# Window attention and SiLU MLP on one core: the partition maximum of the later chunks by a DRAM line instead of GpSimd, and other step times for the folded blocks

## The chip, the cores and the metric

The kernel runs on one core of one Trainium2 chip. The metric is the device time of one execution in microseconds (us), as the median of three runs. Engines go by their names in the profile: PE is TensorE's matmul, PEld its weight load, DVE is VectorE, ACT is ScalarE, POOL is GpSimd, SP is SyncE, whose queue issues every transfer here.

## What is computed

```python
# x (4, 4096, 192), weight_gen (4, 4096, 8 heads, 7 taps)
w = softmax(weight_gen, axis=-1)
x_unf = x_pad[:, s + k, :]                      # a causal window of 7 rows, 8 heads of 24 columns
attn = np.einsum('bshk,bskhg->bshg', w, x_unf)  # (16384, 192)
h = attn @ w_in                                 # 192 -> 2048
out = (h * (1 / (1 + np.exp(-h)))) @ w_out      # 2048 -> 192
```

Everything is float32 at the inputs and the output; the matmuls work on pairs of float16 (an upper and a lower part), for which x is scaled by a power of two that is common to all 128 partitions.

## The kernel before

**Blocks and chunks.** The 16384 rows are 128 tiles of 128; four tiles make a block, so there are 32 blocks. The inputs come in ten chunks: chunks 0 and 1 hold one block, chunk 2 two, chunks 3 to 9 four each. Per chunk the kernel loads `xc` and `wc`, makes the softmax weights (`softmax_steps`) and finds the scale: `scale_steps` sums |x| on ACT in four parts into the columns of `xm` (128 partitions x 4), `absmax_over` takes the maximum over all partitions, and `x_scales` and `finish_scales` make small 128x1 tiles of it (`xup`, `inv`, `gup`, `od`) with a few DVE instructions. `absmax_over` has two steps: `over`, a GpSimd `partition_all_reduce` (L177), and `top`, a DVE maximum over the four columns (L184).

**A block.** `prep_steps` makes the weighted sum over the 7 taps: four products and three sums on POOL (three and two before block 7), the others on DVE (products L487, sums L493, tiles `pr`), then one last DVE sum that joins both halves, the float16 upper part on ACT (L460) and the lower part on DVE (L463, tile `xs`), and a transposition and two half swaps by DMA (`turned`, L470 and L455). PE then makes the first layer into PSUM (`banks`), ACT the SiLU (L732) and the upper float16 part (L743), DVE the lower part (L747, called lower here), both into a ring of 15 (`ringed`); PE makes the second layer out of the ring (L786, L790), and in blocks from 7 on ACT (L684) and POOL (L685, L686) finish each tile of the output.

**Folded blocks.** From block 7 (`FOLD`) a part of the first layer is made with fewer products out of sums: sums of the weights, made once (`fold_w`, L577 to L587, the tiles named `v_out` and `v_in`), and sums of the weighted x, made for every block (`fold_x`: four on POOL, L603, an upper part on ACT, L606, a lower part on DVE, L609, and a transposition, L613). A folded block has two halves, n = 0 and n = 1. In each, PE runs `fold_1` for two pairs of banks, `tile_sums` (second layer), `plain`, `fold_2`, `fold_3`, and `plain`; DVE adds three pieces after `fold_1` (`joined`, L677), a fourth after `fold_2`, without which `fold_3` (L656, the 18 matmuls with `v_in` and `xt` or `xu`) may not start, and makes four lowers: of the last pair of the half before, of z after the fourth joined, and of x and y.

**What sets the order.** All engines run their instructions in the order in which the program issues them. The main loop issues the matmuls, SiLUs and lowers; all the preparation is a list of steps with due times, and `drain(u)` issues whatever is due up to unit u. A block has 16 units, so a unit is some 1.94 us. The table `START` gives the due times: the steps of block b count from u0 = 16 (b - 2), those of a chunk from the u0 of its first block. A folded block drains at its units 0, 1, 2, 3, 5, 6, 7 and 8, 9, 10, 11, 13, 14, 15, so a step due at 12.5 is issued at 13.

- `any_x`: four parts of |x|, `over`, `top`, `x_scales`, the rest of the scales (chunks 4 to 9; `first_x` is the one of chunk 3).
- `fold_v`: DVE product, product, sum, product, sum, joining sum, then ACT upper, DVE lower, transposition.
- `fold_p`: POOL product, product, sum, product, sum, product, sum.
- `fold_s`: the four sums of `fold_x`, upper, lower, transposition. `fold_w`: fetch, four POOL sums, then five pairs of upper and lower.

Of the kernel before, what the change touches and what calls it, by code (L numbers as in the profile page):

```python
# [10 lines left out]
F32 = mybir.dt.float32  # L11
# [3 lines left out]
ALU = mybir.AluOpType  # L15
AX = mybir.AxisListType

P = 128
# [27 lines left out]
    "b2v": (13.1,) * 1 + (13.2,) + (13.3,) * 3 + (13.4,) * 4 + (13.45,) + (19,) + (21,) * 2 + (23, 23, 23),  # L46
    "first_s": (-2, 1, 4, 6.2, 6.5, 8.5),
    "first_x": (-4, -1, 1, 9, 9.25, 18, 19, 20),
    "any_s": (-32, -32, -23, -16, -14, -10),
    "c4s": (-32, -32, -19, -16, -13, -10),  # L50
    "any_x": (-39, -30, -15, -6, -4.5, 3, 4, 5),
    "early": (-5, -41),
    "b3v": (11, 11, 13, 13, 15, 17, 17, 18, 19, 20.5, 20.5, 21, 21, 22.5, 23, 23),
    "b4v": (10, 12, 13, 14.5, 16, 17, 18.5, 20, 22.5, 23, 23),
    "any_p": (11.25,) * 5,
    "any_v": (11, 11.5, 13, 14, 15, 17, 18.5, 20, 22.5, 23, 23),
    "fold_v": (8, 9, 10, 12, 14, 16, 17, 19, 19),
    "fold_p": (1, 3, 5, 7, 9, 11, 13),
    "fold_s": (16.5, 16.5, 16.5, 16.5, 18, 20, 20),
    "fold_w": (36, 44, 45, 46, 47, 50, 52, 53, 55, 58, 60, 61, 63, 64, 65),  # L60
    "prep": (12.5,),
    "load": (0,),
}
# [14 lines left out]
FOLD = 7  # L78
# [6 lines left out]
def kernel(  # L85
# [19 lines left out]
    nc = tc.nc  # L105
# [35 lines left out]
    sm_p = ctx.enter_context(tc.tile_pool(name="sm", bufs=2))  # L141
# [29 lines left out]
    def absmax_over(m, name):  # L171

        got = {}

        def over():
            got["mb"] = sm_p.tile([P, 4], F32, tag="mb", name=f"mb_{name}")
            nc.gpsimd.partition_all_reduce(got["mb"][:, 0:m.shape[1]], m, P, bass_isa.ReduceOp.max)  # L177

        def top():
            if m.shape[1] == 1:  # L180
                got["all"] = got["mb"][:, 0:1]
                return
            r = sm_p.tile([P, 1], F32, tag="ra", name=f"ra_{name}")
            nc.vector.tensor_reduce(out=r, in_=got["mb"][:, 0:m.shape[1]], op=ALU.max, axis=AX.X)  # L184
            got["all"] = r

        return got, [over, top]

# [4 lines left out]
    def x_scales(got, c):  # L193

        p2 = sc_p.tile([P, 1], I32, tag="p2", name=f"p2_{c}")
        down = sc_p.tile([P, 1], F32, tag="xdown", name=f"xdown{c}")
        up = sc_p.tile([P, 1], F32, tag="xup", name=f"xup{c}")
        bits(p2, got["all"].bitcast(I32), EXPONENT, ALU.bitwise_and)
        bits(down, p2.bitcast(F32), FLOOR, ALU.max, 1.0 / TOP_X, ALU.mult)
        nc.vector.reciprocal(out=up, in_=down)  # L200
        sc[c, "down"], sc[c, "up"] = down, up
# [132 lines left out]
    def load_x(c):  # L334
        t0, n = chunks[c]
        rows = HALO + n
        if c != 1:
            t = xc_p.tile([P, CT + HALO, D], F32, tag="xc", name=f"xc{c}")
        if t0 == 0:

            cut = (P - 1) // 16 * 16
            cuts = (HALO, HALO - 2, TB // 2, 0)

            def halo(hi, lo):
                nc.sync.dma_start(out=t[1:1 + cut, lo:hi, :], in_=xf[0:cut, T - HALO + lo:T - HALO + hi, :])
                nc.sync.dma_start(out=t[1 + cut:P, lo:hi, :], in_=xf[cut:P - 1, T - HALO + lo:T - HALO + hi, :])
            nc.sync.dma_start(out=t[:, HALO:rows, :], in_=xf[:, 0:n, :])
            for hi, lo in zip(cuts[:-2], cuts[1:-1]):  # L350
                halo(hi, lo)
            step["halo"] = lambda: halo(*cuts[-2:])
            nc.gpsimd.memset(t[0:1, 0:HALO, :], 0.0)

            def zeros(lo, hi):
                for q in (PB, 2 * PB):
                    nc.gpsimd.memset(t[q:q + 1, lo:hi, :], 0.0)
                q = 3 * PB
                row = t[q:q + 1, lo:hi, :].rearrange("p t d -> p (t d)")
                nc.scalar.activation(out=row, in_=zero[q:q + 1, 0:1].to_broadcast([1, (hi - lo) * D]), func=AF.Copy)  # L360
            step["zeros"] = zeros
            x_t[1] = t[:, TB:, :]
        elif c == 1:
            t = x_t[1]
            nc.sync.dma_start(out=t[:, HALO:rows, :], in_=xf[:, t0:t0 + n, :])
        else:
            nc.sync.dma_start(out=t[:, 0:rows, :], in_=xf[:, t0 - HALO:t0 + n, :])
        x_t[c] = t

    def load_w(c, queue=nc.sync):  # L370
        t0, n = chunks[c]
        t = wc_p.tile([P, CT * H, K], F32, tag="wc", name=f"wc{c}")
        queue.dma_start(out=t[:, 0:n * H, :].rearrange("p a k -> p (a k)"),
                          in_=wf[:, t0:t0 + n, :].rearrange("p t a -> p (t a)"))
        w_t[c] = t
# [32 lines left out]
    def scale_steps(c, absmax):  # L408
        t0, n = chunks[c]
        parts = n // TB  # L410
        rows = n + HALO
        cuts = [rows * i // parts for i in range(parts + 1)]
        m = sm_p.tile([P, 4], F32, tag="xm", name=f"xm{c}")

        def part(i):
            def f():
                part = x_t[c][:, cuts[i]:cuts[i + 1], :].rearrange("p t d -> p (t d)")
                if c in SUMMED:
                    abs_sum(part, m[:, i:i + 1])
                    return  # L420
                nc.vector.tensor_reduce(out=m[:, i:i + 1], in_=part, op=ALU.max, axis=AX.X,
                                        apply_absolute_value=True)
            return f

        got, chain = absmax(m[:, 0:parts], f"x{c}")

        def small():
            x_scales(got, c)

        return [part(i) for i in range(parts)], chain + [small]  # L430
# [4 lines left out]
    def finish_scales(c):  # L435
        inv = sc_p.tile([P, 1], F32, tag="inv", name=f"inv{c}")
        gup = sc_p.tile([P, 1], F32, tag="gup", name=f"gup{c}")
        bits(inv, sc[c, "down"], wsc["down", "I"], ALU.mult)
        bits(gup, sc[c, "up"], wsc["up", "I"], ALU.mult, gtop(c) / TOP_X, ALU.mult)
        sc[c, "inv"], sc[c, "gup"] = inv, gup  # L440

    def out_scale(c):
        od = sc_p.tile([P, 1], F32, tag="od", name=f"od{c}")
        bits(od, sc[c, "inv"], wsc["down", "O"], ALU.mult, TOP_X / gtop(c), ALU.mult)
        sc[c, "od"] = od
# [64 lines left out]
    def abs_sum(v, out):  # L510
        nc.scalar.activation(out=junk_of(v.shape[1]), in_=v, func=AF.Abs, accum_out=out)
# [340 lines left out]
    def at(u, f):  # L852
        todo.append((u, len(made), f))
        made.append(f)
# [7 lines left out]
    def chain(name, fs, u0=0):  # L862
        steps = START[name][-len(fs):]
        for u, f in zip(steps, fs):
            at(u0 + u, f)

    win, wout = moe_w_in.bitcast(I32), moe_w_out.bitcast(I32)
    with tc.manual_schedule():
# [94 lines left out]
        def x2_size():  # L963
            abs_sum(x_t[2][:, 0:HALO + chunks[2][1], :].rearrange("p t d -> p (t d)"), xs2)
            got, (over, top) = absmax_over(xs2, "x2")
            over()
            step["z2"] = lambda: (top(), x_scales(got, 2), finish_scales(2), out_scale(2))
# [21 lines left out]
        for c in range(2, NC):  # L989
            u0 = (chunks[c][0] // TB - 2) * NF  # L990

            def load(c=c):
                if c > 2:
                    load_w(c)
                load_x(c)
            at(START["load"][0] if c == 2 else (chunks[c - 1][0] // TB - 1) * NF + 1, load)

            def prepare(c=c, u0=u0):
                steps = softmax_steps(c, nc.vector if c == 3 else nc.gpsimd)
                parts, more = scale_steps(c, absmax_over)  # L1000
                more.append(lambda: (finish_scales(c), out_scale(c)))
                which = "any_" if chunks[c - 1][1] == CT else "first_"
                chain("c4s" if c == 4 else which + "s", steps, u0)
                chain(which + "x", parts + more, u0)
            if c > 2:
                at(u0 + START["early"][chunks[c - 1][1] == CT], prepare)
# [10 lines left out]
        for b in range(2, NB):  # L1017
            u0 = (b - 2) * NF

            def prep(b=b, u0=u0):  # L1020
                fold = b >= FOLD
                pool, steps, last, more = prep_steps(b, 0 if b < 4 else 4 if fold else 3, fold)
                if b > 2:
                    chain("fold_p" if fold else "any_p", pool, u0)
                chain("fold_v" if fold else f"b{b}v" if b < 5 else "any_v", steps + last, u0)
                if fold:
                    chain("fold_s", more, u0)
            at(START["prep"][0] if b == 2 else u0 - 1, prep)
# [90 lines left out]
        last = (FOLD - 1, NP - 1)  # L1119
        for b in range(FOLD, NB):  # L1120
            for n in range(2):
# [31 lines left out]
                last = (b, NQ + 2 * n + 1)  # L1153
# [6 lines left out]
        for v in range(NP * (NB - 1), NP * NB):  # L1160
            b, p = pairs[v]
# [41 lines left out]
```

## Time and profile before

| | |
|---|---|
| median of 3 runs | 1094.44 us (1093.11 to 1096.25) |
| the profiled execution | 1095.73 us |
| its span, first to last instruction | 1093.9 us |
| busy: PE, DVE, ACT, POOL | 94%, 76%, 75%, 56% of the span |
| mean granted TensorE clock | 0.975 of full speed |

The profiled execution is 1.3 us longer than the median, and 1.8 us of it lie outside the span. Busy shares are averages over the start, 25 folded blocks and the end, whose limits differ.

### The profile page before, as it was taken

Reading aid. Unit: us, or ns where it says so; the run is one execution under the profiler, and the core shown is the slowest. Engines: PE = TensorE matmul, PEld = TensorE weight load, DVE = VectorE, ACT = ScalarE, POOL = GpSimd, SP = SyncE. Lnnn points to the kernel's source line nnn. Section 1 sums busy time; section 2 is a strip of 40 time slices with the busy share of each in tenths; the row PEclk is TensorE's granted clock in tenths of the full one; section 3 lists DMA queues with packets and bytes.
Section 4 is the critical chain, followed back from the end, with each engine's and each line's share of the span. In section 5 each row is a group of like instructions: output and inputs, shape, how many; then the busy total and the mean of one; then the engine's idle time right before and its main releaser. Section 6 shows DMA issues by size and latency. Waiting matters only on the chain.

```text
span 1093.9 us, 32481 instructions
## 1 busy us (share of the span) xinstructions
PE 1033.5 (94%) x14392; PEld 732.2 (67%) x14392; DVE 836.6 (76%) x905; ACT 822.7 (75%) x875; POOL 611.8 (56%) x532
## 2 busy tenths in 40 slices
PE   9999899989997999979999799997999969999998
PEld 7798677657674666646666466664666647666666
DVE  8889777768885887948878488785797848888653
ACT  7988577657985779857798478985789847777774
POOL 1000633567774678756687566874667747667320
PEclk9999999989998999989999899998999989999999
DMA  9442311225220252203432046220442302223200
GB/s 243 136 141 65 132 31 46 45 57 160 64 47 25 57 160 64 53 20 72 145 64 65 8 89 128 64 64 17 122 94 57 64 20 53 65 56 65 65 16 23
DMA packets 103335, 81.06 MB, mean 74 GB/s; under 512 B 78749, under 2 KB 93722, under 8 KB 102170
## 3 DMA queue, kind: packets, MB, share of 16 engines
q1 hardware_dynamic: 103194, 78.99, 29.5%
q8 instruction: 112, 1.84, 0.7%
q14 instruction: 29, 0.24, 0.1%
HBM read 27.85 MB, written 12.58 MB: 37 GB/s over the span
## 4 chain that ended last, share of the span: by engine, by line
PE 68%; DVE 15%; ACT 7%; issue 7%; POOL 2%; POOLq 0%; DVEq 0%; ACTq 0%
PE banks L720 21%; PE banks L786 16%; PE banks L656 12%; PE banks L790 8%; PE banks L761 5%; DVE ringed L747 4%; DVE banks L677 4%; ACT banks L732 4%; DVE pr L493 3%; ACT ringed L743 3%; DVE pr L487 2%; PE banks L711 2%; PE banks L773 2%; DVE xv L677 1%; POOL pr L493 1%
## 5 line engine op out<-in xcount | busy, mean ns | idle before, releaser
L790 PE MATMUL banks<-wo,ringed 64*128 64x192 f16 x3312 | 408.5, 243 | 40.8 <-DVE ringed L747 40.8
L786 PE MATMUL banks<-wo,ringed 64*128 64x384 f16 x3312 | 421.0, 323 | 0.0
L747 DVE SCALAR_TENSOR_TENSOR ringed<-banks,gup,ringed 128x1024 f16<-128x1024 f32 x248 | 317.0, 1279 | 105.4 <-ACT ringed L743 104.9
L732 ACT ACTIVATE banks<-banks,inv 128x1024 f32<-128x1024 f32 x248 | 269.0, 1085 | 112.0 <-PE banks L720 87.2
L743 ACT ACTIVATE ringed<-banks,gup 128x1024 f16<-128x1024 f32 x248 | 276.1, 1113 | 7.9
L720 PEld LDWEIGHTS <-w 64*128 64x128 f16 x2664 | 150.7, 96 | 133.3 <-issue 26.5
L786 PEld LDWEIGHTS <-ringed 64*128 64x128 f16 x3312 | 176.1, 94 | 90.8
L685 POOL TENSOR_TENSOR v_in<-v_in 128x384 f32<-128x384 f32 x100 | 103.2, 1032 | 197.7 <-ACT v_in L684 197.7
L790 PEld LDWEIGHTS <-ringed 64*128 64x128 f16 x3312 | 176.1, 94 | 48.9 <-DVE ringed L747 42.7
L720 PE MATMUL banks<-xt,w 64*128 64x512 f16 x1332 | 192.9, 388 | 11.6 <-DVE ringed L747 11.4
L487 POOL TENSOR_TENSOR pr<-xc,wc 128x768 f32<-128x768 f32 x109 | 171.2, 1573 | 36.4 <-DVE pr L493 28.6
L720 PE MATMUL banks<-xu,w 64*128 64x512 f16 x1332 | 191.4, 386 | 0.0
L493 POOL TENSOR_TENSOR pr<-pr,pr 128x768 f32<-128x768 f32 x81 | 161.5, 1994 | 49.0 <-issue 43.1
L493 DVE TENSOR_TENSOR pr<-pr,pr 128x768 f32<-128x768 f32 x105 | 123.6, 1177 | 57.9 <-POOL pr L493 56.4
L677 DVE TENSOR_TENSOR banks<-banks,xv 128x512 f32<-128x512 f32 x150 | 104.0, 694 | 66.1 <-PE banks L656 60.5
L684 ACT ACTIVATE v_in<-banks,od 128x768 f32<-128x768 f32 x100 | 89.6, 896 | 69.7 <-PE banks L790 67.5
L487 DVE TENSOR_TENSOR pr<-xc,wc 128x768 f32<-128x768 f32 x108 | 137.5, 1277 | 0.2
L656 PE MATMUL banks<-xu,w 64*128 64x256 f16 (+1 forms) x600 | 135.7, 324 | 0.5 <-DVE ringed L747 0.3
L656 PE MATMUL banks<-xt,w 64*128 64x256 f16 (+1 forms) x600 | 135.7, 324 | 0.0
L656 PEld LDWEIGHTS <-w 64*128 64x128 f16 x1500 | 103.8, 95 | 31.6
L656 PEld LDWEIGHTS <-v_in 64*128 64x128 f16 x1200 | 85.3, 95 | 31.9 <-issue 8.6
L686 POOL TENSOR_TENSOR o<-v_in 128x192 f32<-128x192 f32 x100 | 100.8, 1008 | 7.9
(123 smaller groups left out, 978.2 us busy)
## 6 DMA issues: line engine op xcount, KB each, us to landing
xc<-in_x_dram SPq DMA_DIRECT2D x7, 2112.0 KB, 9.7
xu<-xt SPq DMA_DIRECT2D x62, 192.0 KB, 2.9
out_dram<-o SPq DMA_DIRECT2D x61, 192.0 KB, 2.3
v_out<-v_out SPq DMA_DIRECT2D x50, 128.0 KB, 2.5
wc<-in_weight_gen_dram SPq DMA_DIRECT2D x7, 448.0 KB, 4.0
ringed<-in_moe_w_out_dram SPq DMA_DIRECT2D x8, 384.0 KB, 9.3
ringed<-in_moe_w_in_dram SPq DMA_DIRECT2D x14, 192.0 KB, 8.4
xc<-in_x_dram SPq DMA_DIRECT2D x1, 1344.0 KB, 10.1
```

Source lines behind the costliest of these rows:

```text
L487: eng.tensor_tensor(out=pr[k].rearrange("p t (h g) -> p (t h) g", g=G), in0=xin, in1=wv, op=ALU.mult)
L493: eng.tensor_tensor(out=pr[k], in0=pr[k], in1=pr[l], op=ALU.add)
L656: nc.tensor.matmul(h, w, x, start=start, stop=False, skip_group_check=True)
L677: nc.vector.tensor_tensor(out=to, in0=quarter[:, :, in0], in1=kept[:, :, in1], op=ALU.add)
L685: nc.gpsimd.tensor_tensor(out=s[:, 0], in0=s[:, 0], in1=s[:, 1], op=ALU.add)
L686: nc.gpsimd.tensor_tensor(out=o[:, t], in0=s[:, 0, 0:D], in1=s[:, 0, D:2 * D], op=ALU.add)
L720: nc.tensor.matmul(h[:, i], w16[rows, part, p, g], x_in[rows, :, k, :], start=n == 0, stop=n == NT9 - 1)
L732: nc.scalar.activation(out=h, in_=h, func=AF.Silu, scale=sc[chunk_of[b], "inv"])
L743: nc.scalar.activation(out=g_t[b, p][:, 0], in_=h_t[b, p], func=AF.Copy, scale=sc[chunk_of[b], "gup"])
L747: nc.vector.scalar_tensor_tensor(out=g[:, 1], in0=h_t.pop((b, p)), scalar=sc[chunk_of[b], "gup"], in1=g[:, 0], op0=ALU.mult, op1=ALU.subtract)
L786: nc.tensor.matmul(acc_t[b, t, i], gh_t[b, f][rows, t * P:(t + 1) * P], wo16[rows, place(f)], start=f == 0, stop=False, skip_group_check=True)
L790: nc.tensor.matmul(acc_t[b, t, i][:, 0, :], gl_t[b, f][rows, t * P:(t + 1) * P], wo16[rows, place(f), 0], start=False, stop=False, skip_gr ...
```

## The change

For chunks 3 to 9 the maximum over partitions no longer uses GpSimd. SP writes `xm` (128 x 4 floats) to a line in DRAM, and a second transfer reads the whole line of 512 floats back into every partition (`ml`); `top` is a DVE maximum over those 512. In `any_x` the step `top` stands 17.5 units behind `over`, and not 7.5 as before. Chunks 1 and 2 keep GpSimd. The other edits are due times; block 7 gets a list of its own (`fold_1`) for what `fold_v` lists for the later ones. `fold_w`'s POOL sums go from units 44 to 47 to units 58 to 66, its upper and lower parts from 50 to 65 to 81 to 95.

```diff
-    "any_s": (-32, -32, -23, -16, -14, -10),
+    "any_s": (-32, -32, -23, -15, -14, -10),
-    "any_x": (-39, -30, -15, -6, -4.5, 3, 4, 5),
+    "any_x": (-39, -31, -13, -5.5, -4.0, 13.5, 13.5, 15),
-    "fold_v": (8, 9, 10, 12, 14, 16, 17, 19, 19),
-    "fold_p": (1, 3, 5, 7, 9, 11, 13),
-    "fold_s": (16.5, 16.5, 16.5, 16.5, 18, 20, 20),
-    "fold_w": (36, 44, 45, 46, 47, 50, 52, 53, 55, 58, 60, 61, 63, 64, 65),
+    "fold_1": (9, 9, 11, 13, 14, 14, 14, 19, 19),
+    "fold_v": (5, 7, 9, 11, 12.5, 14.5, 17, 19, 19),
+    "fold_p": (0.5, 3.5, 5, 7, 9, 11, 14),
+    "fold_s": (14.5, 16.5, 16.5, 16.5, 18, 23, 23),
+    "fold_w": (36, 58, 60, 62, 66, 81, 81, 84, 86, 87, 88, 90, 93, 94, 95),
...
+    lines = ctx.enter_context(tc.tile_pool(name="line", bufs=2, space=bass.MemoryType.DRAM))
+    def absmax_by_line(m, name):
+        got = {}
+        def over():
+            line = lines.tile([P, 4], F32, tag="line", name=f"line_{name}")
+            n = m.shape[1]
+            got["all_of"] = sm_p.tile([P, P, 4], F32, tag="ml", name=f"ml_{name}", bufs=1)
+            nc.sync.dma_start(out=line[:, 0:n], in_=m)
+            nc.sync.dma_start(out=got["all_of"].rearrange("p q n -> p (q n)"),
+                              in_=line.rearrange("q n -> (q n)").partition_broadcast(P))
+        def top():
+            got["all"] = sm_p.tile([P, 1], F32, tag="ra", name=f"ra_{name}")
+            nc.vector.tensor_reduce(out=got["all"], in_=got["all_of"].rearrange("p q n -> p (q n)"), op=ALU.max, axis=AX.X)
+        return got, [over, top]
...
-                parts, more = scale_steps(c, absmax_over)
+                parts, more = scale_steps(c, absmax_over if c < 3 else absmax_by_line)
...
-                chain("fold_v" if fold else f"b{b}v" if b < 5 else "any_v", steps + last, u0)
+                chain("fold_1" if b == FOLD else "fold_v" if fold else f"b{b}v" if b < 5 else "any_v", steps + last, u0)
```

On POOL, at the place of chunk 5's maximum (end of block 9), before: `mb` is the all-reduce's result, `pr_0` POOL's running sum, and a bare ISA row sets GpSimd's configuration.

```order
L685 TENSOR_TENSOR v_in<-v_in 128x384
L686 TENSOR_TENSOR o_5032<-v_in 128x192
L487 TENSOR_TENSOR pr_1_4923<-xc_1779,wc_1777 128x768
L177 ISA
L177 ISA mb_x_5351<-xm_4145 128x4
L493 ISA
L493 TENSOR_TENSOR pr_0_4922<-pr_0_4922,pr_1_4923 128x768
L685 TENSOR_TENSOR v_in<-v_in 128x384
L686 TENSOR_TENSOR o_5032<-v_in 128x192
```

The same place after the change:

```order
L508 TENSOR_TENSOR pr_1_4931<-xc_1779,wc_1777 128x768
L514 TENSOR_TENSOR pr_0_4930<-pr_0_4930,pr_1_4931 128x768
L706 TENSOR_TENSOR v_in<-v_in 128x384
L707 TENSOR_TENSOR o_5037<-v_in 128x192
L624 TENSOR_TENSOR v_out<-pr_2_4932 128x2x64
```

The all-reduce and the two configuration rows are gone; the sum of `pr_0` follows its product at once.

On DVE, in half n = 0 of a folded block, where no step of a chunk lies between, from the last two joined (L677) to the first step of half n = 1, before: `pr_2` and `pr_3` are DVE's product tiles, `xs` the lower part of x, `v_out` that of the sums.

```order
L677 TENSOR_TENSOR banks<-banks,xv 128x2x256 x2
L463 SCALAR_TENSOR_TENSOR xs_3877<-pr_2_3875,xup_3545,xs_3877 128x4x192
L747 SCALAR_TENSOR_TENSOR ringed<-banks,gup_3555,ringed 128x1024
L609 SCALAR_TENSOR_TENSOR v_out<-v_out,xup_3545 128x2x256
L747 SCALAR_TENSOR_TENSOR ringed<-banks,gup_3555,ringed 128x1024 x2
L487 TENSOR_TENSOR pr_2_4400<-xc_1779,wc_1777 128x768
```

The same after the change (L698 is joined, L768 a lower, L508 a product, L630 the lower part of the sums):

```order
L698 TENSOR_TENSOR banks<-banks,xv 128x2x256 x2
L484 SCALAR_TENSOR_TENSOR xs_3879<-pr_2_3877,xup_3868,xs_3879 128x4x192
L768 SCALAR_TENSOR_TENSOR ringed<-banks,gup_3881,ringed 128x1024
L508 TENSOR_TENSOR pr_2_4408<-xc_1779,wc_1777 128x768
L768 SCALAR_TENSOR_TENSOR ringed<-banks,gup_3881,ringed 128x1024 x2
L630 SCALAR_TENSOR_TENSOR v_out<-v_out,xup_3868 128x2x256
L508 TENSOR_TENSOR pr_3_4409<-xc_1779,wc_1777 128x768
```

The first product stands where the lower part of the sums stood, between the lowers of z and x, and that part has moved behind the lower of y.

On DVE, in half n = 1 of the same block, from the lower of the last pair to the lower of y, before:

```order
L747 SCALAR_TENSOR_TENSOR ringed<-banks,gup_3555,ringed 128x1024
L677 TENSOR_TENSOR banks<-banks,xv 128x2x256
L677 TENSOR_TENSOR xv<-banks,xv 128x2x256
L677 TENSOR_TENSOR banks<-banks,xv 128x2x256
L487 TENSOR_TENSOR pr_3_4401<-xc_1779,wc_1777 128x768
L493 TENSOR_TENSOR pr_2_4400<-pr_2_4400,pr_3_4401 128x768
L677 TENSOR_TENSOR banks<-banks,xv 128x2x256
L747 SCALAR_TENSOR_TENSOR ringed<-banks,gup_3555,ringed 128x1024
L487 TENSOR_TENSOR pr_3_4401<-xc_1779,wc_1777 128x768
L747 SCALAR_TENSOR_TENSOR ringed<-banks,gup_3555,ringed 128x1024
L493 TENSOR_TENSOR pr_2_4400<-pr_2_4400,pr_3_4401 128x768
L747 SCALAR_TENSOR_TENSOR ringed<-banks,gup_3555,ringed 128x1024
```

After the change:

```order
L768 SCALAR_TENSOR_TENSOR ringed<-banks,gup_3881,ringed 128x1024
L698 TENSOR_TENSOR banks<-banks,xv 128x2x256
L698 TENSOR_TENSOR xv<-banks,xv 128x2x256
L698 TENSOR_TENSOR banks<-banks,xv 128x2x256
L514 TENSOR_TENSOR pr_2_4408<-pr_2_4408,pr_3_4409 128x768
L698 TENSOR_TENSOR banks<-banks,xv 128x2x256
L508 TENSOR_TENSOR pr_3_4409<-xc_1779,wc_1777 128x768
L768 SCALAR_TENSOR_TENSOR ringed<-banks,gup_3881,ringed 128x1024
L514 TENSOR_TENSOR pr_2_4408<-pr_2_4408,pr_3_4409 128x768
L768 SCALAR_TENSOR_TENSOR ringed<-banks,gup_3881,ringed 128x1024 x2
L514 TENSOR_TENSOR pr_2_4408<-pr_2_4408,pr_0_4406 128x768
```

A product has gone from ahead of the fourth joined (the fourth L677, now L698) to half n = 0; the third product stands ahead of the lower of z, and only a sum is left between the lowers of z and y.

## Rows read from the trace of the kernel before

**Rows 1.** Stretches: length, busy of PE, PEld, DVE, ACT, POOL; granted clock; DMA, GB/s.

```profile
344.20:378.00 33.80, 26.03 (x326) 16.19 (x328) 23.54 (x28) 18.64 (x19) 23.12 (x20) 0.85 0.22 52
378.00:411.80 33.80, 33.69 (x473) 23.09 (x470) 28.53 (x28) 27.41 (x29) 22.24 (x20) 1.00 0.44 130
...
351.90:357.40 5.50, 5.50 (x36) 2.47 (x38) 1.90 (x3) 2.35 (x3) 5.42 (x7) 0.50 0.10 36
```

**Rows 2.** POOL in order of time, end of block 9: start us, us, what, idle before.

```profile
332.00 1.54 POOL L487 TENSOR_TENSOR pr<-xc,wc 128x768 f32<-128x768 f32 x1
339.37 0.39 POOL L177 PARTITION_ALL_REDUCE mb_x<-xm  x1 [5.83 <-ACT v_in L684]
347.04 1.79 POOL L493 TENSOR_TENSOR pr<-pr,pr 128x768 f32<-128x768 f32 x1 [7.29 <-issue]
```

**Rows 3.** Waits: who for whom, us in total, times, longest.

```profile
DVE pr L493 <- POOL pr L493: 56.4, 6, 10.3
...
PE banks L790 <- DVE ringed L747: 40.8, 5, 8.6
...
PE banks L720 <- DVE ringed L747: 11.4, 3, 4.8
...
ACT v_in L583 <- POOL v_out L577: 5.8, 1, 5.8
```

**Rows 4.** Chain that ended last, folded blocks: start us, us, what.

```profile
270.12 1.80 PE banks L656 x18
...
374.09 1.80 PE banks L656 x18
...
405.15 1.80 PE banks L656 x18
...
1006.68 1.80 PE banks L656 x18
...
1034.05 1.94 PE banks L720 x18
...
1064.67 1.94 PE banks L720 x18
```

**Rows 5.** The same chain, before the folded blocks.

```profile
135.86 3.64 PE banks L720 x18
...
223.66 4.03 PE banks L720 x18
```

**Rows 6.** DVE in order of time, both halves of a folded block.

```profile
392.32 1.10 DVE L609 SCALAR_TENSOR_TENSOR v_out<-v_out,xup 128x512 f16<-128x512 f32 x1
...
395.13 1.28 DVE L747 SCALAR_TENSOR_TENSOR ringed<-banks,gup,ringed 128x1024 f16<-128x1024 f32 x1 [0.52 <-ACT ringed L743]
...
402.85 1.63 DVE L493 TENSOR_TENSOR pr<-pr,pr 128x768 f32<-128x768 f32 x1
404.41 0.69 DVE L677 TENSOR_TENSOR banks<-banks,xv 128x512 f32<-128x512 f32 x1
```

**Rows 7.** All DVE products and sums: duration ns least, median, most.

```profile
L487 DVE TENSOR_TENSOR pr<-xc,wc x108: 937/952/2584, 21.4 to 1008.4; 128x768 f32<-128x768 f32 x108
...
L493 DVE TENSOR_TENSOR pr<-pr,pr x105: 893/958/2449, 23.9 to 1013.9; 128x768 f32<-128x768 f32 x105
```

**Rows 8.** DVE groups: count, busy us, mean ns of one, idle before.

```profile
L384 DVE TENSOR_REDUCE wm<-wc 128x128 f32<-128x896 f32 x7 | 7.5, 1074 | 0.0
...
L184 DVE TENSOR_REDUCE ra_x<-mb_x 128x1 f32<-128x4 f32 x7 | 1.0, 149 | 0.0
```

**Rows 9.** Transfers: count, KB each, median us from issue to landing.

```profile
xu<-xt SPq DMA_DIRECT2D x62, 192.0 KB, 2.9
...
v_out<-v_out SPq DMA_TRANSPOSE x25, 3.6
...
xc<-in_x_dram SPq DMA_DIRECT2D x3, 22.5 KB, 3.2
```

**Rows 10.** DVE in order of time, before the folded blocks.

```profile
200.70 4.58 DVE L487 TENSOR_TENSOR pr<-xc,wc 128x768 f32<-128x768 f32 x2
```

## The prediction

> **What bounds the kernel now.** I read the stretches first, to see where PE is not busy. In the second stretch of [rows 1] PE is busy 33.69 of 33.80 us at a granted clock of 1.00: there matmuls are the bound. In the first, as long and next to it, PE is busy 26.03 us and the clock is 0.85. The reader is to see that the kernel is PE-bound except in stretches that come back once per chunk. The waits say who stops PE in them: the matmuls of the second layer waited 40.8 us in five waits for DVE's lowers, and the first layer 11.4 us in three [rows 3].
>
> POOL in order of time shows why DVE is late [rows 2]. POOL ends a product at 333.5, stands 5.83 us, runs the all-reduce in 0.39 us, stands another 7.29 us in which it waited for nothing that the profile shows ("issue"), and begins its running sum at 347.04: 13.5 us for 0.39 us of work, with a configuration row on either side of it in the order. DVE's joining sum needs that running sum; DVE waited so six times, 56.4 us in all, at most 10.3 [rows 3]. DVE is in order, so the lowers and joined pieces behind the sum wait too, and the ring and PSUM run dry for PE. After PE's gap the granted clock is 0.50, the 1.2 GHz level, in the stretch from 351.90 to 357.40 [rows 1], which makes the gap dearer than its length.
>
> The chain prices all that without my having to add gaps and clock. Between 374.09 and 405.15 the same piece of `fold_3` comes back after 31.06 us: an undisturbed block. From 270.12 to 1006.68, 22 blocks later, it took 736.56 us, and 22 x 31.06 = 683.3, so **the five maxima in between cost 53.2 us** [rows 4]. Before the folded blocks the three gaps are 11.4 us, and two first-layer groups behind them took 3.64 and 4.03 instead of 1.94 us [rows 3 to 5], another 3.8: **15.2 us** around the maxima of chunks 3 and 4.
>
> **The change, part by part.**
>
> *The all-reduce and both reconfigurations leave POOL's queue for chunks 3 to 9.* In the order POOL's sum now follows its product at once, so the 13.5 us go and with them the five disturbances: -53.2 us. Of the early 15.2 us not all comes back. One part was a wait of ACT for `fold_w`'s POOL sums (5.8 us, [rows 3]), which stood behind chunk 3's maximum; the sums now have 15 units or more to the first use. But some DVE work there is merely crowded: two products in one piece took 4.58 us [rows 10] instead of twice 0.95, and five lower parts of `fold_w` move into that stretch. I leave 3 us of the 15.2 there (bounds 0 and all 15.2), an estimate: about one such excess of 4.58 - 1.9 = 2.7 us. So -12.2 us.
>
> *The way through DRAM is added.* The write is 2 KB in 128 rows, for which the nearest row is the smallest transfer shown, 22.5 KB in 3.2 us; the read-back fills 256 KB, nearest 192 KB in 2.9 [rows 9]. SP has to wait for the first to land before it issues the second, so I take 6 us, 7 at most. `over` is issued at unit 13 of a block and `top` at unit 14 of the next, 17 units or 33 us later (a unit is 31.06 / 16 = 1.94 us). The cover is those 33 us of other blocks' work; without it seven times 6 us would be 42 us. Behind the two transfers SP has only the store of a half block's output, and the next transposition of x is due 6 units (11.6 us) on: cost 0, bound above 0 as long as the trip stays under 11 us.
>
> *`top` is longer.* 512 elements instead of 4: by the row of 896 elements, 1074 ns, some 0.61 us against 0.149 [rows 8], +0.46 us, 3.2 us over seven chunks. Most of it falls in DVE's idle time (28.5 of 33.8 us busy, [rows 1]), but it stands between two lowers; I take +1 us (0 to 3.2).
>
> *Moved steps in n = 1.* At the end of the run, where nothing is left to prepare, two halves take 1064.67 - 1034.05 = 30.62 us [rows 4], the price of the matmuls. The undisturbed block is 0.44 us longer. Part of it is in view: DVE's sum at 402.85 and the fourth joined, which ends at 405.10 [rows 6], stand right before `fold_3` at 405.15. After the change a product less stands ahead of that joined, and one product less between the lowers of z and y. 23 blocks prepare something, so the bounds are 0 and -10.1 us; I take 0.3 us a block, -6.9 us, because the sum keeps its place.
>
> *Moved steps in n = 0.* A product takes the place of the lower part of the sums (1.10 us) ahead of the lowers of x and y, and the lower of y had 0.52 us to spare, waiting for ACT [rows 6]. A product takes 0.95 us at the median and 2.58 at most, a sum 0.96 and 2.45 [rows 7]: I take no loss (bounds: no loss, and 1.0 us per block, the longest product less the part that leaves and the spare).
>
> *The rest costs nothing.* The ACT parts of |x| stay in the same gaps between `keep` and the next SiLU, or move by one drain. The transposition of the sums goes from unit 21 to 23 as issued, and is needed at 32: 17.5 us for a transposition of 3.6 and swaps of 2.9 us [rows 9].
>
> *Sum.* 1095.73 (the profiled run, span and what lies around it) - 53.2 - 12.2 + 0 + 1 - 6.9 = 1024.4. The median of the runs is 1.3 us below that run: **1023 us**.
>
> **A rule against it.** The all-reduce itself is 0.39 us [rows 2]. The Trainium skill, GPSIMD Engine Reference, section 4.1 (Engine selection), gives reductions over partitions to GpSimd and names VectorE as what not to use for them. By that rule the move would gain only the busy time, 7 x 0.39 = 2.7 us, off a queue that isn't the bound, and the time would stay between 1092 and 1094. The trace speaks against it here: the reduction is cheap and what stands around it is dear. That result is part of the second rival below.
>
> **The rivals.**
>
> 1. *DVE gets crowded in n = 0.* For it: products that run beside POOL's already take up to 2.58 us, and POOL no longer pauses 13 us per chunk. If every moved product met that, the lower of y would be about 1.0 us late in each block: 23 us, and nothing is gained in n = 1. Time 1023 + 6.9 + 23 = 1053; with half the blocks 1041. Against it: the median product is 0.95 us, so most meet nothing. 12%.
> 2. *The change doesn't do what it says.* The stops stay because something else ends as late, ACT's four sums of |x| or the softmax, whose steps surround the maximum, and what is gained is POOL's 0.39 us per chunk at most [rows 2]. Then 1092 to 1095. Against it: the three other blocks of each chunk hold the same steps and take 31.06 us. 2%.
> 3. *Slower: DVE becomes the bound of the folded blocks.* It has 28.53 / 33.80 x 31.06 = 26.2 us of work in an undisturbed block [rows 1]. If its three products and three sums of a block all went from their median to their longest, 3 x (2.58 - 0.95) + 3 x (2.45 - 0.96) = 9.4 us [rows 7], the work would be 35.6 us, 4.6 us above the block: 105 us in 23 blocks, 1023 + 6.9 + 105 = 1135. It decides from 71 / 23 = 3.1 us lost per block. Against it: POOL would have to be busy whenever DVE is, and it was busy 22.24 of 33.80 us [rows 1]. 3%.
>
> **How the numbers follow.** 83% for the forecast, whose own range is 1014 to 1032: the low end takes all of 15.2 and 10.1 and no cost of `top` (1095.73 - 1.3 - 53.2 - 15.2 - 10.1 = 1016), and the runs' spread of 2 us; the high end nothing in n = 1 and all 3.2 us. The range up to 1042 takes in rival 1 for half of the blocks. A measurement of this kernel tells about 0.3%, 3.3 us, from no change. Faster by more than that is the forecast and rival 1, 95%; within it is most of rival 2, 2%; slower is rival 3, 3%.
>
> **What would show it.** Right: POOL has one reconfiguration in the run, after chunk 2's maximum, DVE's wait for POOL's sum is gone, PE's waits for lowers fall from 52 us to a few, no stretch at 0.50 after the start, and `fold_3` comes back after 30.6 to 31.1 us in every block. Wrong: lowers that end late behind a product in n = 0, blocks above 31.1 us throughout, or `top` waiting for its transfer.

## The result, and the profile after

The changed kernel takes **1027.51 us** (median of four runs, 1027.18 to 1027.53) against 1093.78 (four runs, 1091.87 to 1096.25) beside it on the same chip: ratio 0.9392, 95% interval 0.9372 to 0.9412. The prediction was 1023 us, range 1014 to 1042. The profiled execution took 1027.18 us; its span is 1025.4 us, the mean granted clock 1.00, PE is busy 99% of the span, DVE 83%, ACT 80%, POOL 61%.

Line numbers behind the insertion are 21 higher than before: joined is L698, a lower L768, products L508, sums L514, the pieces of the folded first layer L677, the plain first layer L741, the second layer L807 and L811. `top` is L206, the small scale steps are L212 and L221.

The same two stretches as in [rows 1], after (same columns):

```profile
344.20:378.00 33.80, 33.09 (x478) 23.63 (x474) 29.17 (x35) 26.03 (x28) 24.26 (x21) 1.00 0.52 143
378.00:411.80 33.80, 33.80 (x480) 22.45 (x478) 28.18 (x28) 29.63 (x31) 27.64 (x23) 1.00 0.25 54
```

PE is busy 33.09 us in the first, not 26.03, and up to the last matmul the granted clock is nowhere below 1.00. POOL in order of time at the end of block 9, the place of [rows 2]:

```profile
334.58 1.54 POOL L508 TENSOR_TENSOR pr<-xc,wc 128x768 f32<-128x768 f32 x1
336.20 2.41 POOL L514 TENSOR_TENSOR pr<-pr,pr 128x768 f32<-128x768 f32 x1
```

The running sum follows its product 0.08 us later; before, 13.5 us lay between them. The waits that answer to [rows 3]:

```profile
PE banks L677 <- DVE ringed L768: 3.5, 5, 0.7
PE banks L741 <- DVE ringed L768: 3.3, 4, 2.1
...
PE banks L677 <- DVE banks L698: 1.1, 5, 0.2
```

DVE's wait for POOL's sum (56.4 us) is gone, and PE's waits for lowers fall from 52.2 to 6.8 us. Two of these three rows are five waits each, one per chunk, in front of the folded matmuls: new, small, and met again below. The chain, where [rows 4] stood:

```profile
304.66 1.80 PE banks L677 x18
...
320.15 1.62 PE banks L677 x18
...
335.46 1.62 PE banks L677 x18
...
350.77 1.62 PE banks L677 x18
...
366.97 1.62 PE banks L677 x18
...
799.79 1.80 PE banks L677 x18
...
996.34 1.94 PE banks L741 x18
```

These rows let the gain be split. An undisturbed block takes 350.77 - 320.15 = 30.62 us, the price of the matmuls; it was 31.06. Four chunks take 799.79 - 304.66 = 495.13 us, 123.78 each, which is 1.30 us above four undisturbed blocks. The 22 blocks that took 736.56 us in [rows 4] take 5 x 123.78 + 2 x 30.62 = 680.1 us now: **-56.4 us**. The last first-layer group of the chain stands at 996.34 instead of 1064.67, -68.33 us, so the start and the end gave **-11.9 us**.

The way through DRAM, and SP's issues of it for chunk 5:

```profile
ml_x<-line_x SPq DMA_DIRECT2D x7, 256.0 KB, 4.1
...
line_x<-xm SPq DMA_DIRECT2D x7, 2.0 KB, 2.6
```

```profile
318.74 0.34 SPq L200 DMA_DIRECT2D line_x<-xm  x1
320.37 0.33 SPq L201 DMA_DIRECT2D ml_x<-line_x  x1
```

At 2.6 + 4.1 = 6.7 us the trip has landed 31 us before `top` asks for it. Where the 1.30 us per chunk go, DVE in order of time shows, first in block 9 and then in block 10 (L416 are the softmax sums, L420 and L421 the step with the reciprocal), and under it PE in order of time at both places:

```profile
301.26 1.08 DVE L416 TENSOR_REDUCE ws<-wc 128x128 f32<-128x896 f32 x1
302.37 0.66 DVE L420 TENSOR_SCALAR ws<-ws 128x128 f32<-128x128 f32 x1
303.06 0.95 DVE L421 RECIPROCAL ws<-ws 128x128 f32<-128x128 f32 x1
303.93 0.67 DVE L698 TENSOR_TENSOR banks<-banks,xv 128x512 f32<-128x512 f32 x1
...
354.95 1.27 DVE L768 SCALAR_TENSOR_TENSOR ringed<-banks,gup,ringed 128x1024 f16<-128x1024 f32 x1
356.14 0.67 DVE L206 TENSOR_REDUCE ra_x<-ml_x 128x1 f32<-128x512 f32 x1
...
357.22 0.16 DVE L221 RECIPROCAL xup<-xdown 128x1 f32<-128x1 f32 x1
357.30 1.28 DVE L768 SCALAR_TENSOR_TENSOR ringed<-banks,gup,ringed 128x1024 f16<-128x1024 f32 x1
```

```profile
304.66 0.27 PE L677 MATMUL banks<-xu,v_in 64*128 64x256 f16 x1 [0.22 <-DVE banks L698]
...
358.64 0.27 PE L677 MATMUL banks<-xu,w 64*128 64x256 f16 x1 [0.71 <-DVE ringed L768]
```

In block 10, 1.16 us of `top` and small steps stand between two lowers, PE waits 0.71 us for the second, and the period is 366.97 - 335.46 = 31.51 us, 0.89 too long. In block 9 three softmax instructions stand ahead of the fourth joined, PE waits 0.22 us for it, and the chunk loses the other 1.30 - 0.89 = 0.41 us.

### The profile page after: what moved, and what is told of

Same layout as the page of the kernel before. It is cut to its first block, busy times and chain, and to the rows that moved or that the text cites. A ratio compares the mean times of both kernels' runs of the same rounds, so it can differ in the third digit from the quotient of the medians.

```text
span 1025.4 us, 32480 instructions
## 1 busy us (share of the span) xinstructions
PE 1011.7 (99%) x14392; PEld 732.4 (71%) x14392; DVE 851.7 (83%) x905; ACT 823.6 (80%) x875; POOL 627.6 (61%) x525
## 4 chain that ended last, share of the span: by engine, by line
PE 90%; DVE 6%; ACT 2%; issue 1%; DMA 0%; DVEq 0%; ACTq 0%
PE banks L741 26%; PE banks L807 24%; PE banks L677 16%; PE banks L811 12%; PE banks L782 6%; PE banks L732 2%; PE banks L794 2%; DVE ringed L768 2%; DVE banks L698 1%; ACT banks L753 1%; ACT ringed L764 1%; DVE pr L508 1%; PE banks L555 1%; DVE ws L416 1%; DVE xv L698 0%
## 5 line engine op out<-in xcount | busy, mean ns | idle before, releaser
L807 PE MATMUL banks<-wo,ringed 64*128 64x384 f16 x3312 | 419.8, 322 | 0.0
L811 PE MATMUL banks<-wo,ringed 64*128 64x192 f16 x3312 | 407.7, 243 | 0.1
L768 DVE SCALAR_TENSOR_TENSOR ringed<-banks,gup,ringed 128x1024 f16<-128x1024 f32 x248 | 315.9, 1277 | 68.3 <-ACT ringed L764 68.2
L508 POOL TENSOR_TENSOR pr<-xc,wc 128x768 f32<-128x768 f32 x109 | 192.0, 1764 | 91.4 <-DVE wc L424 58.9
L807 PEld LDWEIGHTS <-ringed 64*128 64x128 f16 x3312 | 177.8, 94 | 89.3
L741 PEld LDWEIGHTS <-w 64*128 64x128 f16 x2664 | 149.9, 94 | 114.9 <-issue 4.8
L706 POOL TENSOR_TENSOR v_in<-v_in 128x384 f32<-128x384 f32 x100 | 106.1, 1061 | 193.9 <-ACT v_in L705 193.9
L741 PE MATMUL banks<-xt,w 64*128 64x512 f16 x1332 | 185.0, 376 | 3.5 <-DVE ringed L768 3.3
L741 PE MATMUL banks<-xu,w 64*128 64x512 f16 x1332 | 184.9, 376 | 0.0
L811 PEld LDWEIGHTS <-ringed 64*128 64x128 f16 x3312 | 177.7, 94 | 6.3 <-DVE ringed L768 0.4
L514 POOL TENSOR_TENSOR pr<-pr,pr 128x768 f32<-128x768 f32 x81 | 177.2, 2188 | 6.3
L698 DVE TENSOR_TENSOR banks<-banks,xv 128x512 f32<-128x512 f32 x150 | 104.0, 694 | 80.2 <-PE banks L677 74.7
L508 DVE TENSOR_TENSOR pr<-xc,wc 128x768 f32<-128x768 f32 x108 | 150.6, 1398 | 0.2
L677 PE MATMUL banks<-xu,w 64*128 64x256 f16 (+1 forms) x600 | 135.0, 322 | 3.5 <-DVE ringed L768 3.5
L677 PE MATMUL banks<-xt,w 64*128 64x256 f16 (+1 forms) x600 | 135.0, 322 | 0.0
L677 PEld LDWEIGHTS <-w 64*128 64x128 f16 x1500 | 103.9, 94 | 29.5
L514 DVE TENSOR_TENSOR pr<-pr,pr 128x768 f32<-128x768 f32 x105 | 120.2, 1145 | 0.6
L677 PEld LDWEIGHTS <-v_in 64*128 64x128 f16 x1200 | 86.3, 94 | 27.6 <-issue 6.3
L677 PE MATMUL banks<-v_out,v_in 64*128 64x256 f16 x900 | 99.3, 269 | 0.0
```

The lines of the kernel that those rows point to most:

```text
L508: eng.tensor_tensor(out=pr[k].rearrange("p t (h g) -> p (t h) g", g=G), in0=xin, in1=wv, op=ALU.mult)
L514: eng.tensor_tensor(out=pr[k], in0=pr[k], in1=pr[l], op=ALU.add)
L677: nc.tensor.matmul(h, w, x, start=start, stop=False, skip_group_check=True)
L698: nc.vector.tensor_tensor(out=to, in0=quarter[:, :, in0], in1=kept[:, :, in1], op=ALU.add)
L706: nc.gpsimd.tensor_tensor(out=s[:, 0], in0=s[:, 0], in1=s[:, 1], op=ALU.add)
L741: nc.tensor.matmul(h[:, i], w16[rows, part, p, g], x_in[rows, :, k, :], start=n == 0, stop=n == NT9 - 1)
```

## The experiments

The theory: what counts is POOL's 13.5 us per maximum with the engines queued behind it, and it is gone by the way through DRAM alone; the new times give 0.44 us per folded block and take 1.3 us per chunk. The rivals: that it is the new times that moved POOL's sum out of the way; that the cover of the trip isn't needed; that the all-reduce could have stayed on GpSimd elsewhere in its queue.

### The way through DRAM alone, and the times alone

The first kernel is the changed one with all old due times, those of the blocks and of `fold_w` too; the second the changed one with the old maximum on GpSimd.

```diff
-    "any_s": (-32, -32, -23, -15, -14, -10),
+    "any_s": (-32, -32, -23, -16, -14, -10),
-    "any_x": (-39, -31, -13, -5.5, -4.0, 13.5, 13.5, 15),
+    "any_x": (-39, -30, -15, -6, -4.5, 3, 4, 5),
...
```
```diff
-                parts, more = scale_steps(c, absmax_over if c < 3 else absmax_by_line)
+                parts, more = scale_steps(c, absmax_over)
```

> The kernel before with the DRAM line for chunks 3 to 9 and every due time as before. Theory A (the two reconfigurations of GpSimd around each all-reduce are the cost): about 1030 us (1026 to 1036), the five fold_3 periods of 41 us fall to 31.1, the other blocks stay at 31.06. Theory B (the new due times bring a large part of the gain): 1045 us or more, periods above 35 us stay.

> All due times of the change, but GpSimd's all-reduce for chunks 3 to 9. Theory A: DVE's joining sum still waits for POOL's running sum behind the all-reduce, five periods stay near 41 us, the quiet blocks take 30.6 us: 1080 to 1092 us. Theory B: 1065 us or less.

The way alone: **1031.91 us**, ratio 0.9431 (0.9415 to 0.9447). The times alone: **1083.21 us**, 0.9904 (0.9889 to 0.9918). In the second the waits are those of [rows 3] again:

```profile
DVE pr L514 <- POOL pr L514: 56.2, 6, 10.2
...
PE banks L811 <- DVE ringed L768: 38.5, 5, 8.4
```

So the way removes 5.7%, the times alone 1.0%, and the theory holds against the first rival. They don't add up (5.7 + 1.0 against 6.1). The chain of the first kernel shows why:

```profile
290.75 1.80 PE banks L677 x18
321.81 1.80 PE banks L677 x18
352.87 1.80 PE banks L677 x18
```

With the old times every block takes 31.06 us, those with the steps of a chunk too: slower than 30.62, but the 1.30 us per chunk, 6.5 in all, are not there. They come with the new times. The second kernel pays for the steps of a chunk too, but less, some 0.8 us per chunk: 0.4 ahead of the fourth joined and 0.4 at `top`, a maximum over four columns there. And it gains something that the changed kernel can't: in its chain four chunks take 531.05 us (from 315.05 to 846.10), 10.3 us each above four blocks of 30.62, so without these 0.8 us the stop is about 1 us shorter than the 53.2 / 5 = 10.6 us of before. Where no stop is left, that part of the gain isn't there.

### Half of the times

The changed kernel with the old times of the blocks' steps, and with the old times of `fold_w`.

```diff
-    "fold_1": (9, 9, 11, 13, 14, 14, 14, 19, 19),
-    "fold_v": (5, 7, 9, 11, 12.5, 14.5, 17, 19, 19),
-    "fold_p": (0.5, 3.5, 5, 7, 9, 11, 14),
-    "fold_s": (14.5, 16.5, 16.5, 16.5, 18, 23, 23),
+    "fold_1": (8, 9, 10, 12, 14, 16, 17, 19, 19),
+    "fold_v": (8, 9, 10, 12, 14, 16, 17, 19, 19),
+    "fold_p": (1, 3, 5, 7, 9, 11, 13),
+    "fold_s": (16.5, 16.5, 16.5, 16.5, 18, 20, 20),
```
```diff
-    "fold_w": (36, 58, 60, 62, 66, 81, 81, 84, 86, 87, 88, 90, 93, 94, 95),
+    "fold_w": (36, 44, 45, 46, 47, 50, 52, 53, 55, 58, 60, 61, 63, 64, 65),
```

> The changed kernel with the due times of before for the block steps alone (fold_v, fold_p, fold_s, block 7 among them). Theory A: quiet blocks go back from 30.62 to 31.06 us, 22 blocks, less what the two slow blocks of each chunk lose already: 1031 to 1037 us. Rival (these times do nothing, the line alone made the blocks shorter): 1027 to 1028 us, blocks stay at 30.6.

> The changed kernel with the due times of before for the sums of the weights alone (fold_w). Theory A (ACT waited for these sums only because the all-reduce of chunk 3 held POOL up): ACT's wait of 5.8 us doesn't come back, and the five lower parts leave the crowded stretch at 200 us: 1025 to 1028 us. Rival (the sums had to be moved): PE stands several us near 130 us again, 1031 us or more.

With the old block steps: **1042.5 us**, 0.9531 (0.9516 to 0.9545), in the expected direction but 5 us past its end, and slower than all old times together. Its undisturbed blocks take 31.06 us again, as expected (262.03 to 293.09 in its chain). But the next four take 125.79 us (293.09 to 418.88), 1.55 above four of 31.06, and with all old times this excess isn't there: new steps of the chunks and old steps of the blocks get into each other's way. Which of them do is not shown. With the old `fold_w`: **1025.36 us**, 0.9357 (0.9343 to 0.9371), 2.1 us faster than the changed kernel. ACT waits 2.1 us for POOL's sums of `fold_w` there, not 5.8 as before. Moving `fold_w` was not needed.

### The all-reduce on GpSimd, behind the running sum

The kernel before, with `over` issued behind POOL's running sum instead of ahead of it.

```diff
-    "any_x": (-39, -30, -15, -6, -4.5, 3, 4, 5),
+    "any_x": (-39, -30, -15, -6, -2.9, 3, 4, 5),
```

> The kernel before with one due time changed: the all-reduce of chunks 4 to 9 one unit later, behind POOL's running sum instead of ahead of it. Theory A (what costs is what stands behind the two reconfigurations in POOL's queue, DVE's joining sum first of all): that sum no longer waits, POOL's finishing of tiles and its four sums are late instead, the long periods fall from 41 to between 32 and 38 us: 1050 to 1080 us. Rival (13.5 us of POOL are lost wherever they stand): periods stay at 40 us or more, 1088 us or more.

**1074.06 us**, 0.9802 (0.9787 to 0.9817): some 2% back with one number, in the expected range. What is left, in POOL's and ACT's order of time at the end of block 9:

```profile
339.53 0.39 POOL L178 PARTITION_ALL_REDUCE mb_x<-xm  x1 [5.95 <-ACT ringed L764]
346.92 0.98 POOL L706 TENSOR_TENSOR v_in<-v_in 128x384 f32<-128x384 f32 x1 [7.01 <-issue]
```

```profile
350.38 0.72 ACT L627 ACTIVATE v_out<-v_out,xup 128x512 f16<-128x512 f32 x1 [6.92 <-POOL v_out L624]
```

The two pauses are as long as before. DVE's sum no longer stands behind them, but POOL's sums for `fold_x` do, and ACT waits 6.92 us for them with the SiLUs queued behind. At both places tried, a stop of 13 us on POOL finds someone; other places were not tried.

### `top` earlier, and how much cover the trip needs

Four other places of `top` (the sixth number), in the order of the table below; in the first the small steps move with it, in the last `over` too.

```diff
-    "any_x": (-39, -31, -13, -5.5, -4.0, 13.5, 13.5, 15),
+    "any_x": (-39, -31, -13, -5.5, -4.0, 2, 2, 2),
+    "any_x": (-39, -31, -13, -5.5, -4.0, -2.0, 13.5, 15),
+    "any_x": (-39, -31, -13, -5.5, -4.0, -4.0, 13.5, 15),
+    "any_x": (-39, -31, -13, -5.5, -5.0, -5.0, 13.5, 15),
```

> The changed kernel with the maximum over 512 and the scales set at unit 2, where DVE waits for PE, instead of 13.5 between two lowers. Theory A (the 0.9 us that the last block before each chunk's switch loses is DVE's 0.67 us maximum and three small steps ahead of the lower of y): those periods fall from 31.51 to 30.7 us, 1022 to 1025 us in all. Rival (the product ahead of the lower of z makes it late, not the maximum): periods stay above 31.3, 1027 us.

> The changed kernel with the maximum over 512 due at unit -2 instead of 13.5, right behind the two transfers, so that the way through DRAM has no cover. Theory A: DVE waits 4 to 5 us per chunk for the read-back (2.6 us to land the line and 4.1 us to land the copies, less the unit in between), with the lowers behind it; six chunks: 1040 to 1055 us. Rival (the way is cheap even bare): 1028 us.

> The changed kernel, with the maximum on VectorE right behind the transfers in the order, one lower activation ahead of it: at the durations seen, the broadcast lands some 2 us after VectorE reaches the step. Theory, that a wait of VectorE in the second half of a folded block costs TensorE what it exceeds the 0.7 us that VectorE idles before the next lower activations: 1025.7 + 5 x 1.5 to 2.5 = 1033 to 1038 us. Rival, that TensorE has banks enough to run on: 1025 to 1028 us.

> As the run before it, with the maximum one product and one lower activation earlier on VectorE, so that it waits some 5 us for the broadcast with a lower activation behind it. Theory: each us of the wait beyond the slack is lost by TensorE, 1025.7 + 5 x 4.5 to 5.5 = 1048 to 1053 us, which is the price of the trip through DRAM where nothing covers it. Rival, that the wait is taken up: 1026 to 1035 us.

| `top` | us | ratio (95%) |
|---|---|---|
| early, at 2 | 1022.96 | 0.9351 (0.9338 to 0.9365) |
| two lowers behind | 1025.72 | 0.9361 (0.9344 to 0.9377) |
| one lower behind | 1034.97 | 0.9458 (0.9440 to 0.9476) |
| at once | 1048.95 | 0.9581 (0.9560 to 0.9602) |

The first met its expectation: away from the lower of y, `top` costs nothing, 4.55 us for 5 x 0.89. The second missed: 1040 to 1055 was expected, since the trip would stand bare. It didn't. SP and DVE in order of time:

```profile
319.31 0.50 SPq L200 DMA_DIRECT2D line_x<-xm  x1
321.15 0.33 SPq L201 DMA_DIRECT2D ml_x<-line_x  x1
```

```profile
326.11 0.67 DVE L206 TENSOR_REDUCE ra_x<-ml_x 128x1 f32<-128x512 f32 x1
```

What DVE has in its queue ahead of `top` takes until 326.11, 6.8 us after the write was issued; the trip takes 6.7 us at its medians. The expectation counted due times, not the instructions between them. The third and fourth kernel take that cover away, and both met their expectations. DVE in order of time and the waits, first with one lower ahead:

```profile
330.37 0.69 DVE L206 TENSOR_REDUCE ra_x<-ml_x 128x1 f32<-128x512 f32 x1 [1.59 <-DMA ml_x<-line_x]
```

```profile
DVE ra_x L206 <- DMA ml_x<-line_x: 10.9, 6, 2.8
```

and then with `top` at once:

```profile
328.56 0.69 DVE L206 TENSOR_REDUCE ra_x<-ml_x 128x1 f32<-128x512 f32 x1 [4.89 <-DMA ml_x<-line_x]
```

```profile
DVE ra_x L206 <- DMA ml_x<-line_x: 26.9, 6, 5.4
...
PE banks L741 <- DVE ringed L768: 19.8, 8, 3.4
```

Against the kernel with two lowers ahead the medians are 1034.97 - 1025.72 = 9.3 us and 23.2 us up. The waits are those of the profiled executions, and these lie further apart: 10.9 us of waiting cost 1037.31 - 1025.84 = 11.5 us, and 26.9 cost 1048.66 - 1025.84 = 22.8. That is 1.05 and 0.85 us of time per us of DVE's wait. The first is the dearer for its one wait ahead of the folded blocks: it is 2.8 us long, PE waits 3.8 us behind it, and from 208.0 to 214.9 the granted clock is 0.51. So the trip is free from some 7 us of cover on; in the changed kernel it has 36 to 37 for chunks 4 to 9, and 14 for chunk 3.

### The reciprocal behind the fourth joined

The kernel with `top` early, and the reciprocal's step one unit later.

```diff
-    "any_s": (-32, -32, -23, -15, -14, -10),
+    "any_s": (-32, -32, -23, -15, -13, -10),
```

> The run with the early maximum, and the reciprocal of the softmax sum one unit later (13 instead of 14 units before), so that only the sum stands ahead of the fourth joined. Theory A (the 31.02 us blocks lose 0.4 us because 2.7 us of softmax steps stand in a gap of 2.3 us ahead of that joined): these periods fall to 30.6 to 30.7 us, 1020 to 1022 us. Rival (they lose it elsewhere): 31.0 us stays, 1023 us.

**1032.64 us**, 0.9424 (0.9410 to 0.9438): a miss, 9.7 us slower than without the edit. DVE in order of time, in block 9 again, from the fourth joined to the lower of z:

```profile
303.71 0.70 DVE L698 TENSOR_TENSOR banks<-banks,xv 128x512 f32<-128x512 f32 x1 [1.16 <-PE banks L677]
304.32 1.09 DVE L420 TENSOR_SCALAR ws<-ws 128x128 f32<-128x128 f32 x1
305.44 0.95 DVE L421 RECIPROCAL ws<-ws 128x128 f32<-128x128 f32 x1
306.31 1.72 DVE L484 SCALAR_TENSOR_TENSOR xs<-pr,xup,xs 128x768 f16<-128x768 f32 x1
307.95 1.27 DVE L768 SCALAR_TENSOR_TENSOR ringed<-banks,gup,ringed 128x1024 f16<-128x1024 f32 x1
```

The fourth joined is on time and now idles 1.16 us for PE ahead of it; the 2.0 us of the step have gone behind it, where they delay the lower of z, to 307.95 from 306.18 with `top` early alone. PE's waits for lowers in front of L741 and L677 rise to 10.3 us, from 3.3. So ahead of the fourth joined there is room for 1.16 us, and behind it none. The same step of 0.66 + 0.95 us ahead of it, as in the changed kernel, is some 0.4 us too long for that room: the 0.41 us per chunk.

### What beats both

The kernel with `top` early and the old `fold_w`; then the same with the softmax sums at -16, as before the change, so that they stand ahead of the last lower of the half before.

```diff
-    "any_s": (-32, -32, -23, -15, -14, -10),
+    "any_s": (-32, -32, -23, -16, -14, -10),
```

> Two edits that each were faster than the changed kernel, together: the maximum on VectorE and what hangs on it at 2 (alone 1022.96 us), and the old times of the folded weights (alone 1025.36 us). If the one acts on the half blocks of the folded stage and the other on the blocks ahead of it, they add: 1027.5 - 4.6 - 2.1 = 1020.8 us, 1020 to 1022. Rival, that both take away the same idle time of TensorE: 1023 us or more.

> The kernel of the run before it, with the sums of the softmax at -16 again, as before the change: they stand ahead of the fourth lower activation of a half block, where VectorE idles 0.76 us for ScalarE, and the step of the reciprocal stays ahead of the fourth joined partial. Theory, that the 31.02 us periods come from 2.7 us of softmax steps in one place: they fall to 30.62 to 30.9, the time by 0 to 2 us, to 1019 to 1021 us. Rival, that the sums delay the fourth lower activation by 0.3 us and TensorE with it: slower than the run before it by 1 to 5 us.

**1020.83 us**, 0.9326 (0.9312 to 0.9340), and **1019.16 us**, 0.9311 (0.9297 to 0.9324). Both expectations are met: the edits add, and the sums' move gives 1.7 us of the 5 x 0.41 = 2.0. It also brings the step with the reciprocal to a place where its first instruction takes 0.22 us instead of 0.66, so the gain is not that of the 1.08 us of the sums alone. In the chain of the second, 413.44 us lie between these two rows, 13.5 blocks of 30.62 us: over more than three chunks nothing but matmul time is left.

```profile
271.87 1.62 PE banks L677 x18
...
685.31 1.62 PE banks L677 x18
```

## Why the prediction was right

**The five stops in the folded blocks**, 53.2 us predicted: they went whole, as one kernel with the old times and without GpSimd shows (31.06 us in every block).

**The start**, 12.2 us predicted with 3 us left behind: 11.9 us with the end in it, and PE still waits 3.3 us there for lowers, 2.1 of it at one place. The two products in one piece that I had seen are there, but they alone aren't the price. DVE in order of time in the changed kernel, then in the one with the old `fold_w`, and that one's waits (the same wait after the change stands in the second row of the waits above):

```profile
195.69 1.32 DVE L608 SCALAR_TENSOR_TENSOR v_in<-v_out,w_up,v_in 64x256 f16<-64x256 f32 x1
197.02 4.70 DVE L508 TENSOR_TENSOR pr<-xc,wc 128x768 f32<-128x768 f32 x2
```

```profile
195.72 4.58 DVE L508 TENSOR_TENSOR pr<-xc,wc 128x768 f32<-128x768 f32 x2
```

```profile
PE banks L741 <- DVE ringed L768: 1.4, 3, 0.6
```

With the old `fold_w` the pair is still there and no wait is above 0.6 us. The 2.1 us come with the lower part of `fold_w` (L608) that its new times put ahead of the pair. I had counted the five lower parts as crowding, but not that the move itself would cost more than it gave.

**The moved steps**, 6.9 us predicted (0.3 per block): 0.44 us per block, 22 x 0.44 = 9.7 in the stretch. The whole excess over the matmuls went, not two thirds.

**`top`**, 1 us predicted, bounds 0 to 3.2: this term was mis-sized, and past its bound. I charged the 0.5 us by which the maximum grows. But the whole step and three small ones came to a new place, between two lowers, where 1.16 us stand now; it cost 0.89 us in each of five chunks, 4.45 us. The kernel with `top` early gives back 4.55.

**"The rest costs nothing"** was wrong by 5 x 0.41 = 2.0 us: I didn't look at the softmax sums, which the new due time puts right behind the third joined. The kernel with the sums at -16 gives back 1.7.

**The trip**, 6 us and hidden: 6.7 us and hidden; bare, it costs 23 us over six of the chunks.

In the stretch of 22 blocks: -53.2 - 9.7 + 4.45 + 2.0 = -56.4 us, what the chain shows. The prediction had -53.2 - 6.9 + 1 = -59.1, 2.7 us more; 0.3 us were missing at the start, and the 1.3 us that I took off because the profiled run of before was that far above the median, which the one of after isn't: together 4.3 of the 4.5 us between 1023 and 1027.5. The causes and their order of size were right. That the time came out this near is in part luck: the moved steps gave 2.8 us more than I took, `top` and the softmax sums cost 5.5 us more, and the two errors partly cancel.

Of the rivals, DVE's crowding is real in its cause but not in its price. All products on POOL and DVE after the change, least, median and most in ns (the second answers to the first row of [rows 7]):

```profile
L508 POOL TENSOR_TENSOR pr<-xc,wc x109: 1535/1545/2272, 109.2 to 938.1; 128x768 f32<-128x768 f32 x109
L508 DVE TENSOR_TENSOR pr<-xc,wc x108: 941/1352/2478, 21.3 to 938.3; 128x768 f32<-128x768 f32 x108
```

The median product is 1352 ns instead of 952, as the first rival feared, but blocks without a step of a chunk are at 30.62 us: the slack was larger than the one wait of 0.52 us that I judged it by. By the rule of the Trainium skill that I had set against the change (GPSIMD Engine Reference, section 4.1, reductions over partitions on GpSimd and not on VectorE) the way would have gained the 2.7 us that the all-reduce was busy; the trace does not agree: 62 us by the way alone. VectorE makes no reduction over partitions here: the transfers bring all 512 numbers into every partition, and it takes the maximum within each.

## What to carry to other kernels

Price an operation by what stands around it in its queue, not by its own duration: 0.39 us of work stopped POOL for 13.5 us, and everything that stood behind it in order. A detour of 6.7 us through DRAM is cheaper than that wherever 7 us of instructions stand ahead of the reader, and one counts instructions for that, not due times. When a stop is removed, look at every step that the new order puts between two links of the chain, however short: two such places were worth 6 us here.

## What the runs showed of the hardware

GpSimd's pauses around the all-reduce were nearly the same at both places: 5.83 and 7.29 us in [rows 2], 5.95 and 7.01 behind the running sum. The Trainium skill, GPSIMD Engine Reference, section 2.1 (Instruction dispatch), gives about 6 us for the first call of newly loaded code; the first pause agrees, and the trace adds a second one on the way back, each time. The row of the first pause in [rows 2] names an ACT instruction, but the all-reduce had nothing to wait for on ACT. What it reads is the four sums of |x|, and the last of them ended 8.7 us before it began, in ACT's order of time before the change:

```profile
330.50 0.19 ACT L511 ACTIVATION_READ_ACCUMULATOR junk<-xc 128x1 f32 x1
```

A DVE product is held up by POOL in a way that the starts and ends of their instructions show. In the changed kernel 75 of the 108 products start while a POOL instruction has 0.15 us or more left to run, and every one of them ends 0.81 to 0.82 us after that instruction; the other 33 take 0.94 to 0.96 us. One of the 75, POOL's product and DVE's:

```profile
319.57 1.54 POOL L508 TENSOR_TENSOR pr<-xc,wc 128x768 f32<-128x768 f32 x1
```

```profile
319.81 2.11 DVE L508 TENSOR_TENSOR pr<-xc,wc 128x768 f32<-128x768 f32 x1
```

POOL's ends at 321.11 and DVE's at 321.92. Before the change it was 44 of 108, so the median was 952 ns and is 1352 now. The DVE step on 128x128 elements (L420) goes the same way: 0.22 us with POOL idle in the fastest kernel, 0.66 in the changed kernel, where POOL finishes a tile (L706), and 1.09 in the kernel with the reciprocal behind the fourth joined, where POOL runs a product. The Trainium skill, SBUF — State Buffer, section "SBUF: two separate sides", says that VectorE and GpSimd take turns at a pair of ports for whole instructions, if VectorE reads two inputs from SBUF or runs in a faster mode; the 0.81 us behind POOL's end agree with that for the products. Whether the step L420 is of either kind, no run shows.
